# A fused transform and gated feed-forward kernel: the pair stage's order set anew, and the weight sums moved to the last two plain chunks

## The chip, the cores and the metric

The kernel runs on one core of one Trainium2 chip. The metric is the device time of one execution in microseconds. Three runs of the kernel before took 2718.64, 2719.53 and 2728.07 us, median 2719.53; the execution that was profiled took 2719.25 us, and its span, from its first instruction to its last, is 2717.5 us.

## The reference

```python
X = np.fft.rfft(x, axis=1)                       # x: 8 x 3008 x 256, fp32
Yr = Xr @ w_r - Xi @ w_i + b_r
Yi = Xr @ w_i + Xi @ w_r + b_i
Yr = np.sign(Yr) * np.maximum(np.abs(Yr) - 0.01, 0.0)     # Yi alike
y = np.fft.irfft(Yr + 1j * Yi, n=3008, axis=1)
t = y.reshape(24064, 256)
gate = 1 / (1 + np.exp(-(t @ w_gate)))           # 256 x 1536
out = (gate * (t @ w_val)) @ w_out               # 1536 x 256
```

A real Fourier transform along each of 8 sequences, a complex 256 x 256 mix with soft threshold in the frequency domain, the transform back, and a gated feed-forward layer over all 24064 tokens.

## The kernel before

**Numbers.** Products must be nearly exact in fp32. Most operands are therefore split into a high and a low part (type fp32r), and one 128 x 128 x 512 product is three matmuls, high x high, high x low and low x high (`products`, L1130 to 1133). The split costs a copy on ACT (high) and a subtraction on DVE (low) for every operand.

**Stages.** The sequences are transformed in groups of 1, 1, 2, 2 and 2. While the later groups are transformed, the feed-forward layer already runs on the first 4608 tokens, in 9 "plain" chunks of 512 tokens (`ffn`, a list of 9 x 12 units; unit j is chunk j // 12, hidden part j % 12). A unit is `ffn1` (12 matmuls `pg`, `pv`; ACT makes the sigmoid, DVE the product, ACT and DVE split it) and, two units behind, `ffn2` (6 matmuls `po`). The loop at L1045 places the transforms' steps (`side`) between the units by weights. Up to unit 87 all forward transforms and mixes are done (`part` = 108 - 20 = 88); then the transforms' memory (pools `cw` and `p2`, the latter with five 4 KB tiles of the tag `big`) is given up by `fft.close()` and the pool `p4` of the pair stage takes its place. In the last 20 units only inverse transforms are left: `load_v` (L479) loads a tile `vf` on SP's queue, two tiles in turn, `inv_a` multiplies it on PE (`pia`, 64 small matmuls, L502), and L514 stores the tokens to `yd` on SP's queue.

**The pair stage.** The other 19456 tokens go in 19 pairs of 512-token blocks. Each product of 2 x 2 blocks is made with 7 block products in place of 8 (a Strassen-Winograd scheme), for both weights. It needs sums of blocks of the weights and of the tokens:

- `make_t(fp, i)` (L684 to 697) makes the sums of the first weight for one hidden pair: 12 calls, additions on POOL in a scratch tile `tb`, split on POOL into `tr`, stored to the memory tensor `td`.
- `make_s(fp)` (L702 to 720) does it for the second weight: 6 calls, scratch `sa` and `sw`, split into `sr`, stored to `sd`. Scratch and results are tiles of the tag `big`.
- The token sums of a pair (`s1f`, `s2f`, and a difference written over `ypair`) are made on POOL too: by `first_operands` (L756 to 765) for the first pair, by `prepare` (L1189 to 1195) for the others.

The 18 weight steps stand in a list `sums`. The loop takes one after every third unit from unit 34 on, so they lie between the transforms.

In the pair stage a half step k multiplies one pair's operands `xop` with the sums `w1s` (loaded on SP from `td`, 4 buffers `w1s0` to `w1s3`): 7 products into the PSUM tiles `z`, `c` and `b`. ACT and DVE add them up, apply the gate and write `h`. Per 3 hidden pairs, `second` makes sums of `h` on POOL (L1298, and accumulating DMAs at L1292), splits them into `op` (ACT L1309, DVE L1311) and multiplies with `w2s` (loaded on SP from `sd`): 7 x 3 products into `l2z`. A pair is 12 half steps and two `second`: 12 x 7 + 2 x 21 = 126 products, 378 matmuls.

**What sets the order.** Outside the pair stage the framework orders each engine's instructions by its own estimate. Engines, SP's and POOL's DMA queues among them, take their instructions in that order, and a waiting instruction holds back what stands behind it. In the pair stage every instruction is a `Task` with an engine, a duration, a wished time `at` (shifted by an entry of the table `NUDGE`) and a latency. `arrange` (L185) plays the tasks through and emits them in the order in which they started. Tasks with `lock` (additions on POOL and subtractions on DVE that use two operands in SBUF) exclude each other in it: `lock` holds the time at which the last of them ended.

```python
starts = [(max(free[e], t.ready, lock if t.lock else 0.0), t) for t in ts]
...
if sums and j > 3 * NF - 3 and j % 3 == 1:
    sums.pop(0)()
```

The first three `w1s` (`load_w1`), the first pair's tokens (`load_y`) and `first_operands` are placed in the last plain chunk; the rest of the pair stage is placed by `arrange`.

Of the kernel before, what the change touches and what calls it, by code (L numbers as in the profile page):

```python
# [9 lines left out]
F32 = mybir.dt.float32  # L10
# [27 lines left out]
LAST_GAP, SIDE_GAP = 20, 3  # L38
PRE = 1
# [73 lines left out]
class Task:  # L113

    def __init__(self, eng, dur, at, fn, deps=(), lat=0.0, lock=False):
# [21 lines left out]
    ),  # L137
    "load": (
        230.81,
    ),  # L140
    "prepare": (
        -336.85, 397.58, 483.22, 32.48, 566.91, 83.5, 531.49, 56.76, 198.43, 398.39, 446.08, 4.74, 205.62,
        90.44, 533.23, 718.11, -102.53, 229.74, 96.65,
    ),
# [7 lines left out]
    ),  # L152
# [8 lines left out]
    ),  # L161
# [12 lines left out]
def arrange(tasks):  # L174

    left = {}
    users = {}
    ready = {e: [] for e in ENGINES}
    for t in tasks:
        t.deps = [d for d in dict.fromkeys(sum(t.behind, t.deps)) if d is not None and d is not t]  # L180
        left[t] = len(t.deps)
        for d in t.deps:
            users.setdefault(d, []).append(t)
        if not t.deps:
            t.ready = 0.0  # L185
            ready[t.eng].append(t)
    free = dict.fromkeys(ENGINES, 0.0)
    lock = 0.0
    order = []
    while True:  # L190
        best = None
        for e, ts in ready.items():
            if not ts:
                continue
            starts = [(max(free[e], t.ready, lock if t.lock else 0.0), t) for t in ts]
            first = min(b for b, _ in starts)
            b, t = min(((b, t) for b, t in starts if b <= first + WINDOW), key=lambda p: (p[1].at, p[0]))
            if best is None or b < best[0]:
                best = b, t
        if best is None:  # L200
            break
        b, t = best
        ready[t.eng].remove(t)
        t.start, t.end = b, b + t.dur * (1.0 if t.eng == "PE" else 1.02)
        free[t.eng] = t.end
        if t.lock:
            lock = t.end
        order.append(t)
        for u in users.get(t, ()):
            left[u] -= 1  # L210
            if not left[u]:
                u.ready = max(d.end + d.lat + hop(d, u) for d in u.deps)
                ready[u.eng].append(u)
    assert len(order) == len(tasks)
    return order
# [3 lines left out]
def tile_fft_mix_ffn(ctx: ExitStack, tc, x, w_r, w_i, b_r, b_i, w_one, w_out, mf, mi, mis, fa, ft, out):  # L219
# [457 lines left out]

    def make_t(fp, i):
        f0, f1 = 2 * fp, 2 * fp + 1
        g = nc.gpsimd  # L680
        w = big("tb").rearrange("p (a b) n -> p a b n", a=2)
# [8 lines left out]
        r = p2.tile([P, 4, 2, P], F32R, tag="big", bufs=NBIG, name="tr")  # L690
# [8 lines left out]
    def make_s(fp):  # L699
# [6 lines left out]
        w = big("sw").rearrange("p a n -> p (a n)").rearrange("p (k n) -> p k n", n=P)  # L706
# [9 lines left out]
        for k0, k1 in ((0, 4), (4, 7)):  # L716
            r = p2.tile([P, 4, 2, P], F32R, tag="big", bufs=NBIG, name="sr")[:, :k1 - k0]
# [309 lines left out]
    sums = [lambda fp=fp, i=i: make_t(fp, i) for fp in range(NH) for i in range(2)] + [lambda fp=fp: make_s(fp) for fp in range(NH)]  # L1027
    for j in range(NF, len(ffn)):
# [3 lines left out]
        if sums and j > 3 * NF - 3 and j % 3 == 1:  # L1032
            sums.pop(0)()
        while side and (acc >= side[0][0] or j >= (part if len(side) > n_last else end) - 1):
# [4 lines left out]
            if len(side) == n_last:  # L1039
# [4 lines left out]
                acc = 0.0  # L1044
        if c == NPL - 1:  # L1045
# [115 lines left out]
    def load_weights(k):  # L1161
        here[:] = "load", 0
        t = new_w1()
        w1_of[k] = t, task("SP", 0.5, (k - 1.5) * SLOT,
                           lambda: nc.sync.dma_start(t.get().bitcast(F32), td[k // 2 % NH, k % 2]), writes=[t], lat=7.5)

    def prepare(p):
# [11 lines left out]
        def sum_(at, fn, out, reads, deps):  # L1179
            return task("POOL", 1.5, (base + at) * SLOT, fn, reads=reads, writes=[out], deps=deps, lock=True)  # L1180

        def split(name, at, src, v, deps):
            t = new_x()
            hi = task("ACT", 0.63, (base + at) * SLOT, lambda: a_.copy(t.get()[:, 0], v()), reads=[src], writes=[t], deps=deps)
            lo = task("DVE", 0.69, (base + at) * SLOT + 1.0, lambda: sub(t.get()[:, 1], v(), t.get()[:, 0]),  # L1185
# [17 lines left out]
    def half(k):  # L1203
# [18 lines left out]
        def copied(at, deps):  # L1222
            t = new_tmp()
            return t, on("ACT", 0.6, at, lambda: a_.copy(t.get(), z.get()), [z], [t], deps)  # L1224
# [246 lines left out]
```

## Time and profile before

| what | value |
|---|---|
| median of 3 runs | 2719.53 us |
| the profiled execution, its span | 2719.25 us, 2717.5 us |
| PE, DVE, ACT, POOL busy | 98%, 80%, 63%, 38% of the span |
| last `yc` of the transforms made | 923.1 us |
| last 20 plain units | about 925 to 1029 us |
| first product of the pairs | 1028.9 us |
| one pair, from one wait of PE to the next | 88 us |

All times are microseconds from the start of the span. A row of a timeline gives start, length, engine, line, operation and tiles, and in brackets how long the engine was idle before and what ended that. `SPq` is SP's DMA queue: a row there is the issue of a transfer, not the transfer. A matmul's length in the trace is its way through the array; in a row of x3 the next product starts before the last one's end. A row of a window gives its length, then for PE, PEld (PE's weight loads), DVE, ACT and POOL the busy time and the count of instructions, then PE's granted clock, the share of the DMA engines and GB/s. A row of the groups gives count, busy time and mean, then idle time before and its causes.

### The profile page before, as it was taken

The page shows a single profiled execution, that of the slowest core. Times are in us where ns is not written, and L with a number is a line of the kernel's source. Part 1 is how long each engine was busy: PE and PEld are TensorE (multiplying, and loading weights), DVE is VectorE, ACT ScalarE, POOL GpSimd, SP SyncE. Part 2 cuts the span into 40 slices and gives each one's busy share as a digit, 9 for nine tenths or more (in the row PEclk, how much of TensorE's full clock was granted, in tenths as well). Part 3 has the DMA queues.
Part 4 walks back from the last instruction along what each step waited for, and adds up shares of the span by engine and source line. Part 5 has one row for each costly group of instructions (what it writes and reads, how often), then busy time and mean ns, then how long its engine had stood idle before and what let it go on. Part 6 is the DMA issues. An engine that isn't in the chain of part 4 may idle for free.

```text
span 2717.5 us, 45378 instructions
## 1 busy us (share of the span) xinstructions
PE 2660.2 (98%) x16763; PEld 2179.3 (80%) x16763; DVE 2173.0 (80%) x3100; ACT 1702.5 (63%) x2852; POOL 1046.1 (38%) x963
## 2 busy tenths in 40 slices
PE   9999999999899999999999999999999999999999
PEld 6778888887789888888888778788788788877777
DVE  5778888788788636888888888888888888887886
ACT  4565554554355446776777767776777667776765
POOL 1441012225700013445454455445554545444541
PEclk9999999999899999999999999999999999999999
DMA  9986655776655575787887778787878778777874
GB/s 299 290 284 194 194 150 171 206 213 209 201 162 150 169 225 163 242 264 222 261 257 242 240 243 270 237 253 233 270 238 252 227 256 261 245 239 224 270 228 138
DMA packets 257660, 617.83 MB, mean 227 GB/s; under 512 B 26464, under 2 KB 130656, under 8 KB 257440
## 3 DMA queue, kind: packets, MB, share of 16 engines
q1 hardware_dynamic: 222720, 521.29, 58.2%
q0 software_dynamic: 34608, 93.60, 15.1%
q8 instruction: 133, 2.18, 0.3%
q14 instruction: 87, 0.71, 0.1%
q10 hardware_dynamic: 112, 0.04, 0.0%
HBM read 440.50 MB, written 116.13 MB: 205 GB/s over the span
## 4 chain that ended last, share of the span: by engine, by line
PE 79%; DVE 13%; DMA 5%; issue 2%; ACT 1%; SPq 0%; POOL 0%; DVEq 0%; ACTq 0%; POOLq 0%
PE l2z L1133 17%; PE z L1133 17%; PE c L1133 10%; PE pm L425 5%; PE b L1133 4%; DVE op L1311 4%; PE pb L391 3%; DMA w2s<-sd 2%; PE pia L502 2%; DVE tmp L1227 2%; PE pg L555 2%; PE pg L556 2%; PE po L583 2%; PE pg L557 2%; PE pv L555 2%; PE pv L556 2%
## 5 line engine op out<-in xcount | busy, mean ns | idle before, releaser
L1133 PE MATMUL z<-xop,w1s 128*128 128x512 f32 x2592 | 682.0, 390 | 1.0 <-DMA w1s<-td 0.9
L1133 PE MATMUL l2z<-op,w2s 128*128 128x512 f32 x2331 | 594.4, 391 | 7.2 <-DMA w2s<-sd 5.0
L1133 PEld LDWEIGHTS z<-xop,w1s 128*128 128x128 f32 x2592 | 485.3, 188 | 108.0 <-DVE xop L1185 4.4
L1133 PEld LDWEIGHTS l2z<-op,w2s 128*128 128x128 f32 x2331 | 436.4, 188 | 108.4 <-issue 7.1
L1224 ACT COPY tmp<-z 128x512 f32<-128x512 f32 x684 | 398.1, 588 | 194.9 <-PE z L1133 112.3
L1311 DVE TENSOR_TENSOR op<-h,op 128x1024 fp32r<-128x1024 f32 (+1 forms) x444 | 463.3, 1070 | 39.1 <-ACT op L1309 36.7
L1309 ACT CAST op<-h 128x1024 fp32r<-128x1024 f32 (+1 forms) x444 | 360.3, 836 | 77.9 <-PE l2z L1133 68.7
L1133 PE MATMUL c<-xop,w1s 128*128 128x512 f32 x1296 | 351.4, 393 | 16.8 <-DVE tmp L1227 16.0
L1133 PEld LDWEIGHTS c<-xop,w1s 128*128 128x128 f32 x1296 | 241.0, 188 | 79.6 <-DVE tmp L1227 31.2
L1298 POOL TENSOR_TENSOR t<-h 128x512 f32<-128x512 f32 x111 | 166.2, 1497 | 330.4 <-DVE h L1263 329.3
L1227 DVE TENSOR_TENSOR tmp<-tmp,c 128x512 f32<-128x512 f32 x342 | 231.4, 679 | 26.5 <-ACT tmp L1224 15.6
L1271 POOL TENSOR_TENSOR h<-tmp 128x512 f32<-128x512 f32 x114 | 155.9, 1368 | 223.7 <-ACT tmp L1243 147.8
L1243 ACT ACTIVATE tmp<-tmp 128x512 f32<-128x512 f32 x342 | 215.2, 634 | 40.9 <-DVE tmp L1227 40.7
L1298 POOL TENSOR_TENSOR h<-h 128x512 f32<-128x512 f32 x111 | 183.0, 1649 | 7.2
L425 PE MATMUL pm<-w_sb,xsh 128*128 128x256 f32 x1008 | 184.3, 284 | 0.0
L1133 PE MATMUL b<-xop,w1s 128*128 128x512 f32 x648 | 182.6, 390 | 0.0
L1227 DVE TENSOR_TENSOR c<-tmp,c 128x512 f32<-128x512 f32 x114 | 79.1, 694 | 120.4 <-PE c L1133 120.1
L1292 POOL DMA_DIRECT2D h<-h x148 | 128.1, 900 | 85.0 <-ACT tmp L1224 44.6
L425 PEld LDWEIGHTS pm<-w_sb,xsh 128*128 128x128 f32 x1008 | 152.9, 189 | 0.8 <-ACT xsh L407 0.4
L1133 PEld LDWEIGHTS b<-xop,w1s 128*128 128x128 f32 x648 | 121.7, 188 | 25.5 <-DVE tmp L1227 0.3
L436 ACT CAST yh<-yc 128x512 fp32r<-128x512 f32 x84 | 52.1, 620 | 141.7 <-DVE yc L415 141.6
L425 PE MATMUL pm<-w_sb,xsl 128*128 128x256 f32 x504 | 139.5, 277 | 0.0
(199 smaller groups left out, 4989.3 us busy)
## 6 DMA issues: line engine op xcount, KB each, us to landing
w1s<-td SPq DMA_DIRECT2D x228, 896.0 KB, 6.3
w2s<-sd SPq DMA_DIRECT2D x259, 384.0 KB, 5.2
h<-h POOLq DMA_DIRECT2D x74, 512.0 KB, 7.7
zf<-zd SPq DMA_DIRECT2D x96, 256.0 KB, 3.7
vf<-vd SPq DMA_DIRECT2D x128, 192.0 KB, 4.1
vd<-vz SPq DMA_DIRECT2D x84, 256.0 KB, 2.9
ypair<-yd SPq DMA_DIRECT2D x19, 1024.0 KB, 7.7
out_dram<-acc SPq DMA_DIRECT2D x76, 256.0 KB, 6.0
```

The lines of the kernel that those rows point to most:

```text
L425: nc.tensor.matmul(o, l, r, start=(i == 0), stop=(i == len(mms) - 1))
L555: nc.tensor.matmul(t, wh, yth[:, ct], start=(ct == 0), stop=False)
L556: nc.tensor.matmul(t, wh, ytl[:, ct], start=False, stop=False)
L1133: nc.tensor.matmul(o, ws[i], vs[j], start=first and not i and not j, stop=i == 1, skip_group_check=not first)
L1224: return t, on("ACT", 0.6, at, lambda: a_.copy(t.get(), z.get()), [z], [t], deps)
L1227: return on("DVE", 0.69, at, lambda: add(t.get(), s.get(), o.get()), [x for x in (s, o) if x is not t], [t], deps)
L1243: return on("ACT", 0.64, at, lambda: a_.activation(t.get(), (o or t).get(), AF.Sigmoid), [o] if o else [], [t], deps)
L1271: made[3, q] = on("POOL", 1.5, 16, lambda: g_.tensor_mul(at_h(3), g22.get(), v.get()), [g22, v], [h], [d22, e22], True)
L1292: return [[on("POOL", 0.9, at + q0, lambda q0=q0, q1=q1: g_.dma_start(h.get()[:, dst, q0:q1], h.get()[:, src, q0:q1], accum_op=ALU.add), [ ...
L1298: return [[on("POOL", 1.5, at + q, lambda q=q: g_.tensor_sub(v()[:, q], h.get()[:, a, q], h.get()[:, b, q]), [h], [o], sum((d[q] for d in ...
L1309: hi = on("ACT", 0.2 + 0.43 * n, at - 8 + q0, lambda q0=q0, q1=q1: a_.copy(t.get()[:, 0, q0:q1], v()[:, q0:q1]), [t_in], [t], sum((d[i] fo ...
L1311: lo.append([on("DVE", 0.3 + 0.5 * n, at - 5 + q0, lambda q0=q0, q1=q1: sub(t.get()[:, 1, q0:q1], v()[:, q0:q1], t.get()[:, 0, q0:q1]), [t ...
```

## The change

It has two parts.

1. **The planner and its tables.** `arrange` no longer lets tasks with `lock` exclude each other. It plays in steps of time, and while DVE and POOL both run such a task, DVE goes at 0.47 and POOL at 0.8 of its speed. Durations and latencies are set anew (POOL's 1.5 becomes 1.3, DVE's 0.69 becomes 0.67 or 0.68, a `w1s` load 7.5 becomes 6.5, a `w2s` load 6.5 becomes 5.5), the time from one engine to another is shorter, and all entries of `NUDGE` are new (one row of it is shown below).
2. **The weight sums.** Their scratch and their results are no longer `big` tiles but buffers of the pair stage in `p4`: scratch in turn in `w1s3` and `w1s2`, results in `xop7` and `xop8`. They are made from unit 88 on, when `p4` is there, 18 steps in 15 units.

```diff
+SUMS_IN = 15
 NUDGE = {
...
     "load": (
-        230.81,
+        16.36,
     ),
...
+SHARED = {"DVE": 0.47, "POOL": 0.8}
 def hop(a, b):
     if a.eng == b.eng and not a.lat:
-        return 0.0 if a.eng == "PE" else 0.1
-    return 1.1 * (0.28 if a.eng == "PE" else 0.12)
+        return 0.0 if a.eng == "PE" else 0.05
+    return 1.1 * (0.22 if a.eng == "PE" else 0.07)
 def arrange(tasks):
...
+            first = min(max(t.ready, now) for t in ts)
+            t = min((t for t in ts if max(t.ready, now) <= first + WINDOW), key=lambda t: (t.at, t.i))
...
+        both = all(e in busy and busy[e][0].lock for e in SHARED)
+        rate = {e: SHARED[e] if both and e in SHARED else 1.0 for e in busy}
...
+    turns = [0]
+    def scratch():
+        turns[0] += 1
+        return p4.tile([P, 7 * 2 * P], F32, tag=f"w1s{2 + turns[0] % 2}", bufs=1, name="sums")
+    def rounded(k):
+        return p4.tile([P, 4, 2, P], F32R, tag=f"xop{7 + k}", bufs=1, name="hilo")
     def make_t(fp, i):
-        w = big("tb").rearrange("p (a b) n -> p a b n", a=2)
+        w = scratch()[:, :8 * P].rearrange("p (a b n) -> p a b n", a=2, b=2)
...
-        r = p2.tile([P, 4, 2, P], F32R, tag="big", bufs=NBIG, name="tr")
+        r = rounded(turns[0] % 2)
     def make_s(fp):
-        a = big("sa").rearrange("p a n -> p (a n)")[:, :4 * P].rearrange("p (f n) -> p f n", f=2)
+        t = scratch()
+        a = t[:, 8 * P:12 * P].rearrange("p (f n) -> p f n", f=2)
...
-            r = p2.tile([P, 4, 2, P], F32R, tag="big", bufs=NBIG, name="sr")[:, :k1 - k0]
+            r = rounded(k0 // 4)[:, :k1 - k0]
...
     for j in range(NF, len(ffn)):
         c, f = divmod(j, NF)
         ffn[j]()
         acc += rates[j >= part]
-        if sums and j > 3 * NF - 3 and j % 3 == 1:
-            sums.pop(0)()
...
+        if p4:
+            while sums and (n_sums - len(sums)) * SUMS_IN < n_sums * (j - part + 1):
+                sums.pop(0)()
```

**SP's queue in the last plain units.** Before, the first load of `w2s` stands among the loads of `vf` and the stores of `yd` like this (the sums had been stored long before):

```order
L479 DMA vf_12268<-vd7_99 48x1024 x2
L1320 DMA w2s_12995<-sd_102 128x768
L514 DMA yd_104<-yf_12305 128x2x188
L514 DMA yd_104<-yf_12308 128x2x188
L479 DMA vf_12346<-vd7_99 48x1024 x2
L593 DMA out_0_dram<-ot_12340 128x512
L593 DMA out_0_dram<-ot_12343 128x512
```

Now that load stands later in the queue, and the third load of `w1s` (into the buffer `w1s2`), which stood well ahead of this place before, comes after it:

```order
L1339 DMA w2s_12989<-sd_102 128x768
L485 DMA vf_12409<-vd7_99 48x1024
L520 DMA yd_104<-yf_12338 128x2x188
L520 DMA yd_104<-yf_12341 128x2x188
L485 DMA vf_12409<-vd7_99 48x1024
L485 DMA vf_12504<-vd7_99 48x1024
L520 DMA yd_104<-yf_12446 128x2x188
L520 DMA yd_104<-yf_12449 128x2x188
L485 DMA vf_12504<-vd7_99 48x1024
L752 DMA w1s_12752<-td_100 128x1792
L520 DMA yd_104<-yf_12541 128x2x188
L520 DMA yd_104<-yf_12544 128x2x188
```

Behind the `w2s` load stand the loads of the last five `vf` tiles, behind the `w1s` load those of the last three. The `w2s` load reads what the first three `make_s` store; the `w1s` load overwrites the scratch of the eighteenth step.

**POOL in the last plain units.** Before, the last step's stores (`sr` to `sd`) are followed by the four token sums of the first pair, and then by those of the second:

```order
L719 TENSOR_TENSOR sr_11220<-sw_11207,sr_11220 128x3x128
L720 DMA sd_102<-sr_11216 128x4x256
L720 DMA sd_102<-sr_11220 128x3x256
L756 TENSOR_TENSOR s1f_12533<-ypair_12311 128x512
L757 TENSOR_TENSOR s2f_12534<-s1f_12533,ypair_12311 128x512
L761 TENSOR_TENSOR ypair_12311<-ypair_12311 128x512
L765 TENSOR_TENSOR s2f_12534<-ypair_12311,s2f_12534 128x512
L1189 TENSOR_TENSOR s1f_13066<-ypair_12997 128x512
```

Now the sums of the weights (`sums`, split into `hilo`) reach into them; this is the end of the eighteenth step:

```order
L730 TENSOR_TENSOR sums_12734<-sums_12734 128x128
L778 TENSOR_TENSOR ypair_12177<-ypair_12177 128x512
L732 TENSOR_TENSOR sums_12734<-sums_12734 128x128
L735 CAST hilo_12748<-sums_12734 128x3x128
L782 TENSOR_TENSOR s2f_12471<-ypair_12177,s2f_12471 128x512
L736 TENSOR_TENSOR hilo_12748<-sums_12734,hilo_12748 128x3x128
L735 CAST hilo_12744<-sums_12734 128x4x128
L737 DMA sd_102<-hilo_12748 128x3x256
L736 TENSOR_TENSOR hilo_12744<-sums_12734,hilo_12744 128x4x128
L737 DMA sd_102<-hilo_12744 128x4x256
L1208 TENSOR_TENSOR s1f_13058<-ypair_12991 128x512
```

The last two token sums of the first pair (L778, L782) stand inside the last step; the first two (L773, L774) stand inside the third `make_s`. All twelve `make_t` stand ahead of them.

**POOL in the pair stage.** Before, the token sums of the next pair are spread between the sums of `h` (here in the second half of the first pair):

```order
L1292 DMA h_13827<-h_13827 128x1024
L1189 TENSOR_TENSOR s1f_14071<-ypair_13790 128x512
L1194 TENSOR_TENSOR ypair_13790<-ypair_13790 128x512
L1298 TENSOR_TENSOR t1_13901<-h_13827 128x512
L1271 TENSOR_TENSOR h_13827<-tmp_14078,tmp_14116 128x512
L1298 TENSOR_TENSOR h_13827<-h_13827 128x512
L1292 DMA h_13827<-h_13827 128x512
L1190 TENSOR_TENSOR s2f_14196<-s1f_14071,ypair_13790 128x512
```

Now three of the four stand in one run:

```order
L1317 TENSOR_TENSOR h_13369<-h_13369 128x512
L1311 DMA h_13369<-h_13369 128x512
L1208 TENSOR_TENSOR s1f_13801<-ypair_13725 128x512
L1209 TENSOR_TENSOR s2f_13820<-s1f_13801,ypair_13725 128x512
L1213 TENSOR_TENSOR ypair_13725<-ypair_13725 128x512
L1290 TENSOR_TENSOR h_13784<-tmp_13790,tmp_13834 128x512
```

The products of a pair, their number and their sizes stay.

More of the change, by code (lines that the diff above doesn't have):

```diff
@@ L164 @@
 ENGINES = ("PE", "ACT", "DVE", "POOL", "SP")
+SHARED = {"DVE": 0.47, "POOL": 0.8}
 def hop(a, b):
     if a.eng == b.eng and not a.lat:
-        return 0.0 if a.eng == "PE" else 0.1
-    return 1.1 * (0.28 if a.eng == "PE" else 0.12)
+        return 0.0 if a.eng == "PE" else 0.05
+    return 1.1 * (0.22 if a.eng == "PE" else 0.07)
 def arrange(tasks):
[L176 to L179, printed above, removed]
+    left, users = {}, {}
+    waiting = {e: [] for e in ENGINES}
+    busy = {}
+    for i, t in enumerate(tasks):
+        t.i, t.ready = i, 0.0
         t.deps = [d for d in dict.fromkeys(sum(t.behind, t.deps)) if d is not None and d is not t]
@@ L184, in arrange @@
         if not t.deps:
[L185 to L188, printed above, removed]
+            waiting[t.eng].append(t)
+    now = 0.0
     order = []
[L190 to L193, printed above, removed]
+    while len(order) < len(tasks) or busy:
+        wake = []
+        for e, ts in waiting.items():
+            if e in busy or not ts:
                 continue
[L195 to L214, printed above, removed]
+            first = min(max(t.ready, now) for t in ts)
+            t = min((t for t in ts if max(t.ready, now) <= first + WINDOW), key=lambda t: (t.at, t.i))
+            if t.ready > now + 1e-9:
+                wake.append(t.ready - now)
+                continue
+            ts.remove(t)
+            busy[e] = [t, t.dur]
+            t.start = now
+            order.append(t)
+        both = all(e in busy and busy[e][0].lock for e in SHARED)
+        rate = {e: SHARED[e] if both and e in SHARED else 1.0 for e in busy}
+        step = min(wake + [busy[e][1] / rate[e] for e in busy])
+        now += step
+        for e in list(busy):
+            busy[e][1] -= step * rate[e]
+            if busy[e][1] > 1e-9:
+                continue
+            t = busy.pop(e)[0]
+            t.end = now
+            for u in users.get(t, ()):
+                u.ready = max(u.ready, now + t.lat + hop(t, u))
+                left[u] -= 1
+                if not left[u]:
+                    waiting[u.eng].append(u)
     return order
@@ L1027, in tile_fft_mix_ffn @@
     sums = [lambda fp=fp, i=i: make_t(fp, i) for fp in range(NH) for i in range(2)] + [lambda fp=fp: make_s(fp) for fp in range(NH)]
+    n_sums = len(sums)
     for j in range(NF, len(ffn)):
@@ L1179, in sum_ @@
         def sum_(at, fn, out, reads, deps):
-            return task("POOL", 1.5, (base + at) * SLOT, fn, reads=reads, writes=[out], deps=deps, lock=True)
+            return task("POOL", 1.3, (base + at) * SLOT, fn, reads=reads, writes=[out], deps=deps, lock=True)
         def split(name, at, src, v, deps):
             t = new_x()
-            hi = task("ACT", 0.63, (base + at) * SLOT, lambda: a_.copy(t.get()[:, 0], v()), reads=[src], writes=[t], deps=deps)
-            lo = task("DVE", 0.69, (base + at) * SLOT + 1.0, lambda: sub(t.get()[:, 1], v(), t.get()[:, 0]),
+            hi = task("ACT", 0.625, (base + at) * SLOT, lambda: a_.copy(t.get()[:, 0], v()), reads=[src], writes=[t], deps=deps)
+            lo = task("DVE", 0.68, (base + at) * SLOT + 1.0, lambda: sub(t.get()[:, 1], v(), t.get()[:, 0]),
                       reads=[src], writes=[t], deps=[hi], lock=True)
@@ L1223, in copied @@
             t = new_tmp()
-            return t, on("ACT", 0.6, at, lambda: a_.copy(t.get(), z.get()), [z], [t], deps)
+            return t, on("ACT", 0.59, at, lambda: a_.copy(t.get(), z.get()), [z], [t], deps)
         def summed(at, t, s, o, deps):
-            return on("DVE", 0.69, at, lambda: add(t.get(), s.get(), o.get()), [x for x in (s, o) if x is not t], [t], deps)
+            return on("DVE", 0.67, at, lambda: add(t.get(), s.get(), o.get()), [x for x in (s, o) if x is not t], [t], deps)
         q1 = prod(0, z, "a11", "b11", True)
@@ L1266, in half @@
         d11 = summed(3.5, b, s, b, [ds, q2])
-        made[0, q] = on("DVE", 0.69, 4.6, lambda: mul(at_h(0), g11.get(), b.get()), [g11, b], [h], [d11, e11])
+        made[0, q] = on("DVE", 0.67, 4.6, lambda: mul(at_h(0), g11.get(), b.get()), [g11, b], [h], [d11, e11])
         v = new_tmp()
@@ L1335, in result @@
                 if s:
-                    return on("DVE", 0.69, at, lambda: add(t.get(), s.get(), o.get()), [s, o], [t], deps)
-                return on("ACT", 0.6, at, lambda: a_.copy(t.get(), o.get()), [o], [t], deps)
+                    return on("DVE", 0.67, at, lambda: add(t.get(), s.get(), o.get()), [s, o], [t], deps)
+                return on("ACT", 0.59, at, lambda: a_.copy(t.get(), o.get()), [o], [t], deps)
             before = [t.uses[-1]]
             if s:
-                before = [on("POOL", 1.5, at - 1, lambda: g_.tensor_add(t.get(), t.get(), s.get()), [s], [t],
+                before = [on("POOL", 1.3, at - 1, lambda: g_.tensor_add(t.get(), t.get(), s.get()), [s], [t],
                              before + list(deps[:1]), True)]
-            d = on("DVE", 0.69, at, lambda: add(t.get(), t.get(), o.get()), [o], [t], [*deps, *before])
+            d = on("DVE", 0.67, at, lambda: add(t.get(), t.get(), o.get()), [o], [t], [*deps, *before])
             ct, s_ = divmod(j, 2)
@@ L1421, in last_second @@
             t, o = results[p][j], os[2 * s_ + ct]
-            d = on("DVE", 0.69, 90, lambda t=t, o=o: add(t.get(), t.get(), o.get()), [o], [t], [d, t.uses[-1]])
+            d = on("DVE", 0.67, 90, lambda t=t, o=o: add(t.get(), t.get(), o.get()), [o], [t], [d, t.uses[-1]])
             col = T0 + (2 * p + s_) * HW
```

38 lines of the change are left out of this document (19 added, 19 removed), and 37 rows, old and new, of the table NUDGE.

## The prediction

> **What bounds the kernel now.** I read the page first, then the windows, the timeline around the last plain chunks, the waits and one period of the pair stage.
>
> ```profile
> core 0: 2717.5 us, clock 0.992
> ```
> ```profile
> PE 2660.2 (98%) x16763; PEld 2179.3 (80%) x16763; DVE 2173.0 (80%) x3100; ACT 1702.5 (63%) x2852; POOL 1046.1 (38%) x963
> ...
> POOL 1441012225700013445454455445554545444541
> ```
>
> PE is busy for 98% of the span, so time is gained only where it stands still or runs slowly, and lost wherever something new makes it stand. POOL has three empty slices of 68 us, from about 750 to 950 us: the weight sums end before them, and the pair stage begins after them. The change puts the sums at the end of that hole. The timeline says how much room there is: the third and fifth from the end of the plain stage's inverse transforms (`pia`), and the first product of the pairs.
>
> ```profile
> 995.26 1.20 PE L502 MATMUL pia<-ft_sb,vf 48*64 48x47 f32 x64
> ...
> 1006.08 1.15 PE L502 MATMUL pia<-ft_sb,vf 48*64 48x47 f32 x64
> ...
> 1028.93 0.84 PE L1133 MATMUL z<-a,w1s 128*128 128x512 f32 x3
> ```
>
> The next rows are windows (length, then busy time of PE, PEld, DVE, ACT and POOL, clock, DMA): the last plain units, and one pair.
>
> ```profile
> 925.00:1029.00 104.00, 104.00 (x1511) 83.82 (x1510) 34.82 (x48) 43.68 (x85) 8.48 (x6) 1.00 0.75 211
> 1147.80:1235.80 88.00, 86.96 (x379) 70.52 (x379) 74.74 (x97) 62.79 (x104) 44.18 (x33) 1.00 0.79 248
> ```
>
> From 925 to 1029 PE has no gap at all; POOL has 8.5 us of work and DVE 34.8 in 104 us. In a pair, DVE is busy for 75 of 88 us and POOL for 44, so the two overlap, and there PE waits once a pair for DVE:
>
> ```profile
> PE c L1133 <- DVE tmp L1227: 16.0, 17, 1.2
> ```
> ```profile
> 1235.77 0.96 PE L1133 MATMUL c<-xop,w1s 128*128 128x512 f32 x3 [0.92 <-DVE tmp L1227]
> ...
> 1237.94 0.84 PE L1133 MATMUL z<-xop,w1s 128*128 128x512 f32 x3
> 1238.62 0.84 PE L1133 MATMUL b<-xop,w1s 128*128 128x512 f32 x3
> ```
> ```profile
> 1230.73 1.55 DVE L1311 TENSOR_TENSOR op<-h,op 128x512 fp32r<-128x512 f32 x1
> ...
> 1235.64 0.68 DVE L1311 TENSOR_TENSOR op<-h,op 128x512 fp32r<-128x512 f32 x1
> ```
> ```profile
> 1231.80 1.64 POOL L1194 TENSOR_TENSOR ypair<-ypair 128x512 f32<-128x512 f32 x1
> ```
>
> One product is three matmuls and starts 0.68 us after the one before (1237.94 to 1238.62). A pair has 126 of them, 85.7 us; the window, cut from one such wait to the next, has 88.0 (the timeline gives 87.98). So 2.2 us a pair are lost, 42 us in 19 pairs, and no order can win more. The cause is in the last rows: the same DVE subtraction takes 0.68 us alone and 1.55 beside POOL's 1.64 us operation.
>
> **The sums in their new place.** They are the same 18 steps (12 for the first weight, 6 for the second), and each issues its own stores from POOL. What they cost is read where they ran back to back: two steps of the first kind, then two single steps of the second.
>
> ```profile
> 651.09:667.36 16.27, 16.27 (x163) 14.51 (x162) 15.18 (x20) 6.05 (x12) 15.79 (x22) 1.00 0.83 263
> 713.68:723.91 10.23, 4.01 (x70) 3.46 (x70) 8.80 (x10) 1.93 (x4) 10.07 (x15) 0.62 0.41 137
> 723.91:733.53 9.62, 8.31 (x34) 7.17 (x35) 4.64 (x4) 4.28 (x9) 9.47 (x15) 0.69 0.98 268
> ```
> ```profile
> L684 POOL TENSOR_TENSOR tb<-w1h,w1l x24: 729/748/1229, 352.9 to 660.3; 128x256 f32<-128x256 f32 x24
> L692 POOL CAST tr<-tb x24: 397/403/1132, 383.4 to 664.4; 128x256 fp32r<-128x256 f32 x24
> L693 POOL TENSOR_TENSOR tr<-tb,tr x24: 725/745/1225, 384.6 to 666.1; 128x256 fp32r<-128x256 f32 x24
> ...
> L687 POOL TENSOR_TENSOR tb<-tb x12: 454/640/1176, 355.6 to 661.6; 128x128 f32<-128x128 f32 x12
> ```
> ```profile
> L694 POOL DMA_DIRECT2D td<-tr x12 | 6.8, 568 | 3.3 <-POOL tr L693 3.3
> ```
>
> A step of the first kind took 8.1 us with DVE busy for 93% of the time. At the least values of its rows it takes 2 x (0.729 + 0.397 + 0.725) + 4 x 0.454 + 0.57 = 6.1 us, which I take as the price without DVE. DVE is busy for 33% in the last plain units, so I take 6.1 + 2.0 x 33/93 = 6.8. A step of the second kind took 10.2 us (DVE 86%) and 9.6 (DVE 48%); carried on to 33% that is 9.4. In POOL's order the pairs' first four operand sums stand among the last steps:
>
> ```profile
> 969.90 1.29 POOL L756 TENSOR_TENSOR s1f<-ypair 128x512 f32<-128x512 f32 x1 [236.37 <-DMA ypair<-yd]
> 971.26 1.62 POOL L757 TENSOR_TENSOR s2f<-s1f,ypair 128x512 f32<-128x512 f32 x1
> 972.84 1.74 POOL L761 TENSOR_TENSOR ypair<-ypair 128x512 f32<-128x512 f32 x1
> 975.82 1.29 POOL L765 TENSOR_TENSOR s2f<-ypair,s2f 128x512 f32<-128x512 f32 x1 [1.23 <-DVE s L753]
> ```
>
> They add 5.9 us. The whole is 12 x 6.8 + 6 x 9.4 + 5.9 = 144 us, while from the end of the transforms to the pairs there are 106.
>
> The GPSIMD Engine Reference of the Trainium skill (section 3.1) gives 2.6 cycles an element for an addition of two inputs on GpSimd at 1.2 GHz; an estimate from that page is 0.55 us for 256 elements, where the least row here has 0.729. With its figure for the eight two-input operations a first step would be 4.7 us and the sum below 25 us smaller; the measured rows decide.
>
> **When they start, and who waits.** The new buffers lie in memory that the transforms have used, and the first sum can start when the last `yc` is made:
>
> ```profile
> 922.38 0.69 DVE L415 TENSOR_TENSOR yc<-ys,yc 128x512 f32<-128x512 f32 x1
> ```
>
> That is 923.1. Nothing on PE waits for POOL there, but SP does. Its queue goes in order, and in the new order two loads stand in it that need the sums: the first `w2s`, which reads what three steps of the second kind store, and the third `w1s`, whose buffer is the scratch of the last step. Behind the first stand the `vf` loads for the last five inverse transforms (first used at 995.26), behind the second those for the last three (first used at 1006.08), and stores of `yd`. PE's matmuls of `pia` stand in PE's own order and wait for them. Prices:
>
> ```profile
> vf<-vd SPq DMA_DIRECT2D x128, 192.0 KB, 4.1
> ...
> sd<-sr POOLq DMA_DIRECT2D x6, 512.0 KB, 4.4
> ```
> ```profile
> 953.38 0.48 SPq L735 DMA_DIRECT2D w1s<-td  x1
> ...
> 955.71 1.12 SPq L479 DMA_DIRECT2D vf<-vd  x2
> ```
>
> From the issue of a `w1s` load to the end of the `vf` issues behind it SP needs 3.4 us (953.38 to 956.83), and 4.1 more for landing: 7.5 us.
> - First stop: 923.1 + 12 x 6.8 + 3 x 9.4 + 2.9 (two operand sums stand ahead) = 1035.8, + 4.4 for the store, + 7.5 = 1047.7 in place of 995.3: PE stands for 52 us.
> - The next unit takes 5.4 us (half of 995.26 to 1006.08), to 1053; the one after that finds its load behind the third `w1s`.
> - Second stop: the last step's last operation ends at 1035.8 + 3 x 9.4 + 3.0 - 0.8 (its store's issue) = 1066.2; + 7.5 = 1073.7 in place of 1006.1.
>
> So the plain stage ends **67.6 us later**. The stops do not add up; the second deadline contains the first. From below: at 6.1 us a first step it is 59. From above: at 8.1 and 10.2 us, 88. After that nothing of the sums is late: the third `w1s` needs only to land before the pairs start, which is then at 1096, and the operand sums lie ahead of the last step. Half clock after such a stop I put at 2 us (0 to 4): the last two windows above show clock 0.62 and 0.69 around stops of a few us.
>
> What lies under it costs nothing: DVE's 34.8 us in these units, stretched by 1.55/0.68, are 79 of 104. If that cover failed, PE would wait for `hl`, but it uses it two units later.
>
> **What the old place gives back.** There the sums stretched DVE's work and PE stood:
>
> ```profile
> 672.67 1.98 PE L338 MATMUL pd<-xd,ft_sb 47*64 47x512 f32 x6 [2.32 <-DVE yt L427]
> ```
> ```profile
> 716.33 0.55 PE L462 MATMUL pi<-yh,mi_sb 128*128 128x256 f32 x1 [4.55 <-issue]
> ...
> 718.52 0.45 PE L502 MATMUL pia<-ft_sb,vf 48*64 48x47 f32 x2 [0.57 <-DVE yt L427]
> 720.21 1.95 PE L502 MATMUL pia<-ft_sb,vf 48*64 48x47 f32 x62 [1.24 <-issue]
> 724.13 0.58 PE L462 MATMUL pi<-yh,mi_sb 128*128 128x256 f32 x1 [1.97 <-ACT yh L436]
> 725.81 0.58 PE L463 MATMUL pi<-yl,mi_sb 128*128 128x256 f32 x1 [1.10 <-DVE yl L437]
> ```
> ```profile
> 923.78 0.39 PE L462 MATMUL pi<-yh,mi_sb 128*128 128x256 f32 x1 [0.62 <-ACT yh L436]
> 924.50 0.39 PE L463 MATMUL pi<-yl,mi_sb 128*128 128x256 f32 x1 [0.34 <-DVE yl L437]
> ```
>
> The five waits from 716 to 726 are 9.4 us, and the slow clock in the two windows costs 4.01 x 0.38 + 8.31 x 0.31 = 4.1. The same place of the last transforms, with POOL idle, waits for 1.0. So 12.5 us go; of the 2.3 at 672 perhaps most: **-14 us** (-8 if the wait called "issue" stays, -17 if all goes).
>
> **The new order.** The rewritten planner, its durations and tables issue no instruction of their own; a pair keeps its 126 products. The planner's slowing of DVE to 0.47 and of POOL to 0.8 when both run is near the rows: 0.68/1.55 = 0.44, 1.29/1.64 = 0.79. The old planner held one of the two back, which the chip does not do. So the new order should foresee the wait of each pair; shorter hops and load times leave less slack for the DMAs. Nothing in the trace prices an order. It can win at most 42 us, less the products' own hiccups, say 38, and may lose 10 (a new wait of half a us a pair); I take the middle of what can be won, **-20 us**.
>
> **Sum.** 67.6 + 2 - 14 - 20 = +35.6. The profiled execution took 2719.25 us (span 2717.5), 0.3 under the median of 2719.53: **2755 us**.
>
> **Rivals.**
> - *The new order does nothing.* For it: the old one leaves only 2.2 us a pair. Then +55.6: 2775, and with sums at their upper price 2795.
> - *Faster: the sums fit.* With DVE mostly idle POOL's operations could be half as long. It decides when POOL reaches the third step's store by 995.3 - 7.5 - 4.4 = 983.4, 60 us after 923.1 in place of 113, and ends by 998.6, 75 us in place of 143. Then only -34 is left: 2685. Against it: the medians of L684 and L693, 0.748 and 0.745, lie on the least values, 0.729 and 0.725, so waiting for DVE is a small part. By the SBUF — State Buffer page of the Trainium skill ("Who interferes with whom") a DVE operation with two SBUF inputs and a reading GpSimd operation exclude each other for the whole instruction; that would favour this rival. The window from 651 speaks against it: DVE 15.18 and POOL 15.79 busy in 16.27 us.
> - *No change.* Sums at the floor (59), order near its limit (-36), all of the old stalls gone (-17): +6, 2725.
>
> **Numbers.** Forecast 0.62, its own range 2733 to 2770; order without effect 0.21; no change 0.10; faster 0.07. Half a per cent, 13.6 us, is about what a measurement of this kernel tells from no change. Slower by more: 0.83; within it 0.10; faster 0.07. A range from 2728 to 2790 leaves out the faster rival, half of "no change" and the sums at their upper price.
>
> **What would show it.** Right: SP idle for tens of us at the first `w2s` and again at the third `w1s`; PE waiting for `vf` near 995 for some 50 us and near 1053 for some 20; first product of the pairs near 1096; no five waits near 716; a period of about 87 us a pair. Wrong: `pia` waits of under 10 us there, or a pair of 88 us or more.

## The result, and the profile after

The changed kernel took 2752.4 us (median of four runs, 2746.26 to 2756.13), the kernel before 2720.2 in the same comparison (2718.64 to 2728.07): a ratio of 1.0116, with an interval from 1.0097 to 1.0136. It is slower by 32 us; the forecast was 2755. The profiled execution is the quickest of the four, 2746.26 with a span of 2744.4, so the traces lie 26.9 us apart where the medians lie 32.2. The terms below come from the traces.

The head of the page and the slices of POOL and of the clock:

```profile
span 2744.4 us, 45326 instructions
...
PE 2648.9 (97%) x16763; PEld 2182.5 (80%) x16763; DVE 2132.6 (78%) x3100; ACT 1687.9 (62%) x2852; POOL 981.1 (36%) x963
...
POOL 1431000000000992434544455445544455444532
PEclk9999999999999969999999999999999999999999
```

A slice is 68.6 us. POOL's hole now reaches from about 270 to 890 us, and two full slices follow it; in the second of them, 960 to 1029, the clock falls to 0.6.

Four rows of the timeline divide the difference: the last `yc` of the transforms, PE's two long stops behind it (in the second PE waits for a `vf` to land), and the first product of the pairs.

```profile
893.42 0.69 DVE L421 TENSOR_TENSOR yc<-ys,yc 128x512 f32<-128x512 f32 x1
...
992.98 0.79 PE L589 MATMUL po<-hh,w 128*128 128x512 f32 x1 [32.82 <-ACT ot L598]
...
1035.08 0.41 PE L508 MATMUL pia<-ft_sb,vf 48*64 48x47 f32 x2 [12.37 <-DMA vf<-vd]
...
1061.06 1.52 PE L1152 MATMUL c<-s,w1s 128*128 128x512 f32 x6
```

- The last `yc` comes at 893.4 in place of 922.4: the old place gave back **29.0 us**.
- From there to the first product 167.6 us pass in place of 106.5 (1028.93 - 922.38): the new place costs **61.1 us**.
- From the first product to the end of the span 1683.34 us remain in place of 1688.57: the new order is worth **5.2 us**.

-29.0 + 61.1 - 5.2 = 26.9, the difference of the spans.

PE's waits in the pair stage, first before, then after, say why the order is worth so little. (Columns: what waited, for what, total, times, longest.)

```profile
PE l2z L1133 <- DMA w2s<-sd: 5.0, 8, 2.2
```
```profile
PE l2z L1152 <- DMA w2s<-sd: 23.3, 13, 2.4
PE c L1152 <- DVE h L1284: 2.2, 5, 0.9
PE z L1152 <- ACT tmp L1243: 1.7, 4, 0.6
```

The 17 waits for DVE's `tmp`, 16.0 us, are gone, but the waits for the second weight's load grew from 5.0 us to 23.3. All of PE's waits there come to 23.8 us before and 27.9 after, so by these waits alone the new order would be the dearer one. Its 5.2 us stand in PE's busy time, 1650.9 us in place of 1659.1 for the same products; what shortened that is not shown.

### The profile page after: what moved, and what is told of

Its sections match the earlier page's. It is cut to its first block, busy times and chain, and to the rows that moved or that the text cites. A ratio compares the mean times of both kernels' runs of the same rounds, so it can differ in the third digit from the quotient of the medians.

```text
span 2744.4 us, 45326 instructions
## 1 busy us (share of the span) xinstructions
PE 2648.9 (97%) x16763; PEld 2182.5 (80%) x16763; DVE 2132.6 (78%) x3100; ACT 1687.9 (62%) x2852; POOL 981.1 (36%) x963
## 4 chain that ended last, share of the span: by engine, by line
PE 82%; DMA 8%; POOL 5%; DVE 3%; ACT 1%; issue 1%; SPq 0%; DVEq 0%; POOLq 0%; ACTq 0%
PE z L1152 21%; PE l2z L1152 18%; PE c L1152 10%; PE pm L431 6%; PE b L1152 5%; DMA w2s<-sd 4%; PE pb L397 3%; PE pia L508 2%; PE pg L561 2%; DMA ypair<-yd 2%; PE pg L562 1%; PE po L589 1%; PE pv L561 1%; PE pg L563 1%; PE pv L563 1%; PE pv L562 1%
## 5 line engine op out<-in xcount | busy, mean ns | idle before, releaser
L1152 PE MATMUL l2z<-op,w2s 128*128 128x512 f32 x2331 | 608.0, 391 | 23.3 <-DMA w2s<-sd 23.3
L1330 DVE TENSOR_TENSOR op<-h,op 128x1024 fp32r<-128x1024 f32 (+1 forms) x444 | 489.6, 1121 | 73.2 <-ACT op L1328 68.7
L1152 PE MATMUL c<-xop,w1s 128*128 128x512 f32 x1296 | 358.8, 391 | 2.5 <-DVE h L1284 2.2
L1290 POOL TENSOR_TENSOR h<-tmp 128x512 f32<-128x512 f32 x114 | 168.8, 1481 | 375.3 <-DVE tmp L1246 297.9
L700 POOL TENSOR_TENSOR sums<-w1h,w1l 128x256 f32<-128x256 f32 x24 | 18.5, 772 | 618.8 <-DVE yc L421 618.8
L1317 POOL TENSOR_TENSOR t<-h 128x512 f32<-128x512 f32 x111 | 144.2, 1299 | 151.0 <-DVE h L1282 147.0
L1317 POOL TENSOR_TENSOR h<-h 128x512 f32<-128x512 f32 x111 | 155.7, 1403 | 8.7
L1359 POOL TENSOR_TENSOR acc<-acc,tmp 128x512 f32<-128x512 f32 x54 | 90.9, 1683 | 86.4 <-ACT tmp L1348 86.4
```

Source lines behind the costliest of these rows:

```text
L1152: nc.tensor.matmul(o, ws[i], vs[j], start=first and not i and not j, stop=i == 1, skip_group_check=not first)
L1290: made[3, q] = on("POOL", 1.3, 16, lambda: g_.tensor_mul(at_h(3), g22.get(), v.get()), [g22, v], [h], [d22, e22], True)
L1317: return [[on("POOL", 1.3, at + q, lambda q=q: g_.tensor_sub(v()[:, q], h.get()[:, a, q], h.get()[:, b, q]), [h], [o], sum((d[q] for d in ...
L1330: lo.append([on("DVE", 0.13 + 0.555 * n, at - 5 + q0, lambda q0=q0, q1=q1: sub(t.get()[:, 1, q0:q1], v()[:, q0:q1], t.get()[:, 0, q0:q1]), ...
L1359: before = [on("POOL", 1.3, at - 1, lambda: g_.tensor_add(t.get(), t.get(), s.get()), [s], [t], before + list(deps[:1]), True)]
```

## The experiments

Times are medians, against a median of the kernel before on the same chip of 2718.2 us (order_only, place_only, operands_late, one_scratch), 2716.8 (no_sums, split10, split_w1, w1_behind), 2719.4 (split_late, w1_between, both) and 2721.5 (late_fixed).

### The two parts apart

The new order with the sums as they were; and the old order with the sums as they are now:

```
# order_only: the changed kernel, with the loop's lines and both functions as before
+        if sums and j > 3 * NF - 3 and j % 3 == 1:
+            sums.pop(0)()
-        if p4:
-            while sums and (n_sums - len(sums)) * SUMS_IN < n_sums * (j - part + 1):
-                sums.pop(0)()
# place_only: the kernel before, with the same lines the other way round
```

> The changed kernel with the sums of weights in their old place and old buffers: the new order alone. Theory (from the two traces: from the first product of the pairs to the last, 1684.2 us before and 1679.2 after): the order is worth 5 us, so 2720.2 - 5 = 2715; PE's 16.0 us of waits for DVE's tmp are gone, and some 20 us of waits for w2s stand in their place. Rival (the prediction's term): the order is worth 20 us and the profiled runs hide it, 2700. Second rival: the order wins only beside the new place, 2720 or more.

Measured 2714.5, a ratio of 0.9985 (0.9973 to 0.9997). PE's waits in the pair stage:

```profile
PE l2z L1140 <- DMA w2s<-sd: 23.0, 14, 2.0
```

> The kernel before with the sums in their new place and buffers and its old order of the pairs: the move alone. Theory: the old place gives back 28.6 us (the last transforms end that much earlier), the new one costs 60.7, so 2720.2 + 32.1 = 2752, 5 us of which the new order would then win back or which the runs can't tell; I say 2752 to 2757. Rival (the prediction's terms, -14 and +69.6): 2776. PE waits as in the changed kernel: some 33 us near 960 behind an ACT copy, some 12 near 1035 for vf.

Measured 2750.5, just under the 2752 to 2757 that were expected; a ratio of 1.0128 (1.0109 to 1.0148). The waits in the last plain units:

```profile
PE po L584 <- ACT ot L593: 32.4, 1, 32.4
PE pia L503 <- ACT s L764: 10.6, 1, 10.6
```

Order alone -4, place alone +32: the terms of the traces, and neither of the prediction's two, -20 and +55.6 (69.6 - 14). The loss is the move's, and the order brings next to nothing with the old place as with the new.

### Which queue holds PE

The prediction named SP's queue. The trace of after names ACT at the first stop:

```profile
989.75 0.62 ACT L769 CAST s<-s1f 128x512 fp32r<-128x512 f32 x1 [35.69 <-POOL s1f L773]
```
```profile
988.47 1.25 POOL L773 TENSOR_TENSOR s1f<-ypair 128x512 f32<-128x512 f32 x1
...
1024.52 1.27 POOL L736 TENSOR_TENSOR hilo<-sums,hilo 128x512 fp32r<-128x512 f32 x1
```

ACT's copy of the first operand sum stands 35.7 us for POOL, which reaches that sum behind fourteen steps and most of a fifteenth; behind the copy, in ACT's queue, stand the plain stage's copies `ot`, `hh` and `yf`, for which PE waits. The third `w1s` load goes out at 1025.82, when POOL's last operation has ended (1024.52 + 1.27). Two edits were to take away one hold each (a hold is a waiting copy or load that keeps what stands behind it from PE):

```
# one_scratch
-        return p4.tile([P, 7 * 2 * P], F32, tag=f"w1s{2 + turns[0] % 2}", bufs=1, name="sums")
+        return p4.tile([P, 7 * 2 * P], F32, tag="w1s3", bufs=1, name="sums")
# operands_late: the operands' sums and copies are called after the loop
-            if prep and f > 2:
-                prep.pop(0)()
```

> The changed kernel with the copies and sums of the first pair's operands called after the last plain unit in place of within the last chunk; nothing else. Theory (two deadlines, of which the later contains the first): PE's stop of 32.8 us near 960, in which ACT's copy of an operand sum waited for POOL, goes; PE then runs on to a vf load near 972 that SP's queue holds behind the first w2s load until about 995, and the last three vf loads still wait for the third w1s load: the pairs start as before and the time stays at 2752, within 4. Rival: the stops add, 36 us less: 2716.

Measured 2748.8, a ratio of 1.0122 (1.0103 to 1.0140): nothing gained, as the theory had it. ACT's copy no longer stands there, and SP's queue and PE show what stood behind it:

```profile
963.89 0.50 SPq L485 DMA_DIRECT2D vf<-vd  x1
1000.64 0.34 SPq L1337 DMA_DIRECT2D w2s<-sd  x1
```
```profile
1004.86 0.41 PE L508 MATMUL pia<-ft_sb,vf 48*64 48x47 f32 x2 [29.94 <-DMA vf<-vd]
...
1061.55 1.52 PE L1150 MATMUL c<-s,w1s 128*128 128x512 f32 x6
```

This is the prediction's first stop: SP issues nothing for 36 us, until the first `w2s` load can go, and PE waits 29.9 us for the `vf` behind it. It had been in the changed kernel all along, covered by ACT's. The pairs start at 1061.55, within 0.5 us of after.

> The changed kernel with one scratch buffer for the sums (that of the fourth w1s) in place of two, so that the third w1s load no longer waits for the last step; nothing else. Theory (two stops, the second held by that load): the first stop near 960 stays, the second near 1035 goes with its 13.0 us and the 2.9 us of slow clock behind it: 2752.4 - 16 = 2736. Rival: vf is late anyway because the w2s load ahead of it holds SP, or the steps, which can no longer overlap, end later: less than 5 us gained, 2748 or more.

Measured 2755.2, a ratio of 1.0137 (1.0119 to 1.0155): the theory failed. The third `w1s` load went out at 924, but PE stopped again near the end, for ACT, and POOL's last sum came later:

```profile
1036.45 0.62 ACT L769 CAST a<-ypair 128x512 fp32r<-128x512 f32 x1 [18.12 <-DMA sd<-hilo]
```
```profile
1037.49 0.80 PE L561 MATMUL pg<-yth,w1h 128*128 128x512 f32 x1 [10.94 <-ACT yf L519]
```
```profile
1034.21 1.27 POOL L736 TENSOR_TENSOR hilo<-sums,hilo 128x512 fp32r<-128x512 f32 x1
```

The operand `a` goes into one of the two buffers in which the sums are rounded, so its copy waits for the stores of the last step. And with one scratch buffer the steps no longer overlap: POOL ends at 1035.5 in place of 1025.8. That is the second half of the rival; the first, `vf` behind the `w2s` load, cost 5.9 us. The edit changes two things at once, so it doesn't price the third `w1s` load alone. At least four holds lead from POOL's sums to PE: an operand sum and an operand buffer through ACT's queue, a `w2s` and a `w1s` load through SP's. In operands_late, taking one away uncovered the next; in after, place_only, operands_late and one_scratch the pairs start 27 to 37 us after POOL's last sum of the weights.

### What the old place costs

> The new order with the sums of weights left out: copies of the weights are stored where the sums should be, by POOL's queue and without an operation of POOL, so the output is not the reference's. It prices the old place: theory (the last transforms end 28.6 us earlier once the sums are gone from there), 2714.5 - 28.6 = 2686. Rival (the prediction's 12.5 to 17 us, the rest of the 28.6 coming from something else in the move): 2698 to 2702.

```
     def make_t(fp, i):
...
+        for n, f in enumerate((f0, f1)):
+            for v, w in enumerate((w1h, w1l)):
+                g.dma_start(td[fp, i][:, 3 + 2 * n:5 + 2 * n, v], w[:, f, i].bitcast(F32))
```

Measured 2712.3, a ratio of 0.9975 (0.9962 to 0.9989), where 2686 was expected. The total can't decide: the copies went out in the first 210 us, where DMA is at its densest, and delayed PE there by 20.8 us. One matmul ahead of the old place and one behind it, in the run with the new order alone and in this one:

```profile
191.16 0.40 PE L561 MATMUL pg<-yth,w1h 128*128 128x512 f32 x1
...
726.13 0.40 PE L563 MATMUL pg<-yth,w1l 128*128 128x512 f32 x1
```
```profile
211.91 0.40 PE L561 MATMUL pg<-yth,w1h 128*128 128x512 f32 x1
...
721.82 0.39 PE L563 MATMUL pg<-yth,w1l 128*128 128x512 f32 x1
```

A run that was 20.8 us behind at 211 us is 4.3 ahead at the second: the sums cost 25.1 us in their old place. In after, which has the sums elsewhere, that second matmul stands at 701.01, again 25.1 us ahead of order_only, and 28.6 ahead of before (729.60). So some 25 of the 29.0 are the sums', and the rest lies between two traces that both have the sums in the old place; the 12.5 to 17 of the prediction are too few either way.

### Fewer steps late

Ten of the twelve steps of the first kind go back to the old place and its buffers; two and the six of the second kind stay late, with one scratch buffer:

```
+FIRST = 10
...
+        if len(sums) > n_sums - FIRST and j > 3 * NF - 3 and j % 3 == 1:
+            sums.pop(0)()
...
-            while sums and (n_sums - len(sums)) * SUMS_IN < n_sums * (j - part + 1):
+            while sums and (n_sums - FIRST - len(sums)) * SUMS_IN < (n_sums - FIRST) * (j - part + 1):
```

> The new order; the first ten steps of the sums in their old place and buffers, the other eight in the new place with one scratch buffer. Theory (the ten early steps, spaced three units apart, cost little, since before 667 us the kernel before had lost only 8 us by them; POOL then needs 2 x 6.1 + 6 x 8.9 + 5 = 71 us after the transforms, less than the 72 to the first load that would be held and the 106 to the pairs): 2714.5 - 28.6 + 8 = 2694. Rival (operand sums, w2s load and operand buffers still come behind the sums in the queues, so that eight steps hold PE as eighteen do, for about 8/18 of the time): 2686 + 8 + 27 = 2721.

Measured 2724.8, a ratio of 1.0027 (1.0013 to 1.0041). The first half of the theory held (the last `yc` came 20.3 us earlier than with the order alone, 20.6 expected), the second did not: ACT's copy stood for `s1f` again, and PE with it.

```profile
977.03 0.62 ACT L770 CAST s<-s1f 128x512 fp32r<-128x512 f32 x1 [23.55 <-POOL s1f L774]
```
```profile
978.07 0.79 PE L562 MATMUL pg<-yth,w1h 128*128 128x512 f32 x1 [22.07 <-ACT yf L520]
```

> The kernel with ten steps early and eight late, and the copies and sums of the first pair's operands called after the last plain unit. Theory (eight steps are done within 84 us of the end of the transforms, and what held PE for 22.1 us in the run with ten and eight was only ACT's copy of an operand sum, queued ahead of the plain stage's copies): the stop goes, the pairs start near 1008 in place of 1034.9, and 2724.8 - 27 = 2698. Rival (the hold only moves, as with one scratch buffer: to SP's w2s load or to the pairs' first operands): 2712 or more.

The edit is that of operands_late, in this kernel. Measured 2722.0, a ratio of 1.0011 (1.0001 to 1.0020). The theory failed. The edit did not do here what it had done there: called later, the copy kept its place in ACT's queue, since the plain stage's order is the scheduler's.

```profile
980.77 0.62 ACT L770 CAST s<-s1f 128x512 fp32r<-128x512 f32 x1 [26.22 <-POOL s1f L774]
```

### The load that is late in the pairs

With the new order alone, where PE waits for `w2s`: SP's queue, the wait, and the time from the load's issue to its landing.

```profile
1194.36 0.32 SPq L1172 DMA_DIRECT2D w1s<-td  x1
1195.04 0.42 SPq L1327 DMA_DIRECT2D w2s<-sd  x1
1195.55 0.39 SPq L1183 DMA_DIRECT2D ypair<-yd  x1
1196.03 15.07 SPq L1172 DMA_DIRECT2D w1s<-td  x3
```
```profile
1203.65 1.66 PE L1140 MATMUL l2z<-op,w2s 128*128 128x512 f32 x6 [1.54 <-DMA w2s<-sd]
```
```profile
DMA to landing us min/median/max: 8.6/8.6/8.6
```

The first row and the three that follow it within 2 us are four loads, 3.2 MB together (the last row merges three). The `w2s` load lands after 8.6 us, where the new plan counts on 5.5 (the old one had 6.5); the median of all `w2s` loads is 4.2. Two runs move the `w1s` load that stands ahead, in SP's queue alone:

```
         order = arrange(tasks)
+        sp = [t for t in order if t.eng == "SP"]
+        for n in range(2, len(sp)):
+            if [t.load for t in sp[n - 2:n + 1]] == ["w1", "w2", "y"]:
+                order.remove(sp[n - 2])
+                order.insert(order.index(sp[n]) + 1, sp[n - 2])   # w1_between: without + 1
```

> The new order with the sums in their old place, and in SP's queue, at each of the places where w1s, w2s and ypair are loaded within 1.2 us of each other, the w1s load put behind the ypair load; nothing else. Theory (the w2s load takes 8.7 us there in place of 5.5 because the 896 KB of w1s lie ahead of it, and PE waits 1.5 to 2.4 us for it): w2s lands some 3 us earlier, the waits of about 20 us go, 2714.5 - 18 = 2697. Rival (ypair and POOL's own transfers slow it, or something else is late next): within 5 us of 2714.5.

Measured 2704.7, a ratio of 0.9952 (0.9939 to 0.9964). Half of the gain came: the waits for `w2s` are gone, and the load that was moved is late by about 1 us. PE's waits from 1150 to 2600 us:

```profile
PE z L1141 <- DMA w1s<-td: 16.0, 16, 1.8
```

> The new order with the sums in their old place, and the w1s load put between the w2s load and the ypair load in place of behind ypair; nothing else. Theory (each load lands when those ahead of it in the queue have; behind ypair the w1s load came 0.7 to 1.8 us too late at 17 places): w1s lands some 3 us earlier, w2s still in time, the 16.6 us of waits for w1s go: 2704.7 - 14 = 2691. Rival (the four loads share the same bytes a second and one is late in any order): within 5 us of 2704.7, or up to 2714.

Measured 2693.3, a ratio of 0.9904 (0.9890 to 0.9918). With `w2s`, `w1s`, `ypair` in that order the same `w2s` load lands after 5.9 us, and from 1150 to 2600 us no load is late by more than 0.2:

```profile
PE z L1141 <- ACT tmp L1235: 4.4, 12, 0.8
PE z L1141 <- DMA w1s<-td: 0.2, 1, 0.2
```

### A version that beats both

The ten early steps and the `w1s` load behind `ypair` at once (the run split_w1, for which 2676 was expected) measured 2714.1, a ratio of 0.9990 (0.9978 to 1.0001). That is 10.7 below split10, as w1_behind is 9.8 below order_only: the two edits add, but each had brought less than its theory, and ACT's copy still held PE for 21.4 us.

> Both edits at once: ten steps early and eight late with the first operands called last, and the w1s load between w2s and ypair. Theory: they lie in different stages and add: 2714.5 - 16.5 - 23.5 = 2675. Rival (as far as either edit falls back by its own rival): 2690 to 2705.

Measured 2703.2, a ratio of 0.9941 (0.9928 to 0.9954): ten steps early and the `w1s` load between, where 2675 was expected. ACT's copy still stood (22.3 us of PE), so this half was as in split_late, and the load's half held. The last run ties the operands' calls to the last three plain units:

```
+        if j < len(ffn) - LATE:
+            ffn[j]()
+        else:
+            with tc.manual_schedule():
+                ffn[j]()
+                for _ in range(3):
+                    if prep:
+                        prep.pop(0)()
```

> Ten steps early and eight late, the w1s load between w2s and ypair, and the sums and copies of the first pair's operands tied to the last three plain units, so that ACT's copies really stand behind the plain stage's (in the two runs with those calls moved to the end they had kept their place in ACT's queue). Theory (ACT's copy of an operand sum, waiting for POOL's eight steps, is all that held PE there for some 22 us): the stop of 22 us near 955 goes, with 3 us of slow clock behind it; the copies among the last units cost up to 5 us; 2703.2 - 20 = 2683, 10 below the 2693.3 of the run with the sums in their old place and the w1s load between. Rival (SP's first w2s load, which waits for the third step of the second kind and has vf loads behind it, holds PE in ACT's place): 2695 or more.

Measured 2683.1, a ratio of 0.9871 (0.9850 to 0.9893), 10 us below w1_between, which has all the sums in their old place. The copies now come at 1001 us, the stop is gone, and the pairs start at 1008.1:

```profile
1001.45 0.61 ACT L771 CAST a<-ypair 128x512 fp32r<-128x512 f32 x1
```
```profile
PE pia L510 <- DMA vf<-vd: 4.3, 4, 2.7
```
```profile
1008.09 1.52 PE L1161 MATMUL c<-s,w1s 128*128 128x512 f32 x6
```

## Why the prediction was right, step by step

The time and the sign were right, and so was the mechanism of the largest term: the sums don't fit between the transforms and the pairs, and POOL's lateness reaches PE through queues that go in order. Three terms were mis-sized, and their errors largely cancel: the sums 8.5 too dear, the old place 11 to 15 too cheap, the order 15 too good. That the forecast of 2755 lies within 3 us of the median is therefore luck; the traces' 26.9 stands against the sum's 35.6.

- **Sums in the new place, 69.6 with the clock; measured 61.1.** POOL ran from 894.35 to 1025.8, 131 us, where the step had 143. The 12 steps of the first kind took 6.0 us each, the price at the least values, not 6.8 with a share for DVE; the six of the second 9.0, less the operand sums, not 9.4.
- **"Nothing on PE waits for POOL there, but SP does": the step that failed.** The operand sums were counted as POOL's time, but not that ACT copies them and that the plain stage's copies stand behind those. PE stopped at 960, some 12 us ahead of the place that was named (995.3, less the 23 by which PE was early there), and for 36 us, not 52; the stop that was named lay behind it, as operands_late showed.
- **The stops do not add, and the end is set by the end of the last step: right.** With the first stop's cause gone the pairs started at 1061.55 in place of 1061.06. But the third `w1s` load was not the only hold at the end; the operand buffers were another.
- **Clock after the stops, 2 us: too small.** From 993.0, where PE goes on, to 1003.4 the clock is 0.50. In a window table (length, busy PE, PEld, DVE, ACT, POOL, clock, DMA):

```profile
993.00:1000.00 7.00, 3.88 (x31) 2.31 (x34) 7.00 (x5) 1.86 (x4) 6.98 (x13) 0.50 0.57 197
1000.00:1003.40 3.40, 3.40 (x55) 2.92 (x50) 3.01 (x2) 0.36 (x1) 3.40 (x6) 0.51 1.01 266
1003.40:1010.00 6.60, 6.60 (x89) 5.28 (x89) 2.21 (x3) 3.57 (x8) 6.24 (x11) 1.00 1.01 313
```

  PE is busy for 7.3 us of these 10.4, at half speed: 3.6 us lost. Behind the second stop some 3 more go: from 1035.08 to 1045 PE is busy for 9.3 us at a clock of 0.71.
- **The old place, -14; measured -29.0 against before, -25.1 by no_sums and against order_only.** Only the stop at 672 and those from 711 on had been counted, and the slow clock behind the latter alone. The same windows of the kernel before and of after:

```profile
450.00:500.00 50.00, 47.32 (x400) 38.21 (x400) 38.52 (x65) 24.30 (x44) 11.25 (x17) 0.94 0.54 163
650.00:700.00 50.00, 47.51 (x495) 38.10 (x494) 43.76 (x58) 21.37 (x40) 45.79 (x67) 0.93 0.70 221
700.00:750.00 50.00, 40.50 (x399) 35.74 (x397) 38.32 (x52) 18.09 (x32) 31.26 (x48) 0.86 0.65 193
```
```profile
450.00:500.00 50.00, 49.77 (x438) 41.96 (x437) 36.89 (x67) 25.89 (x47) 0.00 (x0) 1.00 0.60 171
650.00:700.00 50.00, 49.49 (x657) 42.66 (x656) 37.42 (x68) 25.04 (x46) 0.00 (x0) 1.00 0.54 156
```

  Standing and clock together, the three windows of before lost 5, 5 and 15 us more than those of after: each of the first two 2 to 2.5 us of standing and some 3 of slow clock, the last 9.5 and 5.7 (in after PE is busy there throughout, at full clock). That is 26 of the 29.
- **The order, -20; measured -5 in the trace and -4 in order_only.** That it takes the DVE wait away was right. The 20 was the middle of a range without a row, and late loads, which the text had named as a risk, took its place: the median pair still takes 88.0 us, the value that the text gave as a sign of being wrong. Whether the shorter load times in the tables or only the order of the loads made `w2s` late, no run separates. With the loads in another order the new plan brought what had been hoped for: w1_between lies 21 us below order_only (2714.5 to 2693.3) and 26 below before.
- **The signs.** Right: the five waits near 716 are gone, and SP issues nothing from 1010.2 until the third `w1s` load at 1025.82. Not so: SP's first long stretch without an issue ends with the store of `ot`, for which ACT's queue was late, and not with the `w2s` load; no wait for `vf` of 50 us came near 995, and the pairs start at 1061 and not near 1096.
- **The faster rival** needed POOL's operations at half their time. They ran at the least values of before and no lower. The Trainium skill's SBUF — State Buffer page ("Who interferes with whom"), which spoke for it, has issue order decide which of the two engines blocks. The trace of operands_late doesn't bear that out: DVE paid, though its subtraction began at 1019.66, ahead of three of the POOL operations that it stood through (1019.81, 1021.03 and 1021.97; last section).

## What to carry to other kernels

Before moving work to an idle engine, list every instruction of the other engines that waits for it, and for each what stands behind it in its own queue: an ACT copy and a DMA load that nobody needs yet can hold work that is needed at once. Sum the work against the hole first; if it doesn't fit, moving less of it may, once the waiting copies stand late (split10 lost, late_fixed won). And price a stall with the slow clock behind it, and a planned load with what is issued beside it.

## What was not expected of the hardware

A DVE operation can stand through several of POOL's. In operands_late the subtraction that takes 0.68 us alone took 3.46 and 3.32, and each time ended only in a pause of POOL, while POOL issued a store:

```profile
1019.66 3.46 DVE L770 TENSOR_TENSOR s<-s1f,s 128x512 fp32r<-128x512 f32 x1 [48.31 <-ACT s L769]
1023.04 3.32 DVE L770 TENSOR_TENSOR s<-s2f,s 128x512 fp32r<-128x512 f32 x1
```
```profile
1019.81 1.25 POOL L774 TENSOR_TENSOR s2f<-s1f,ypair 128x512 f32<-128x512 f32 x1
1021.03 0.98 POOL L736 TENSOR_TENSOR hilo<-sums,hilo 128x384 fp32r<-128x384 f32 x1
1021.97 0.60 POOL L735 CAST hilo<-sums 128x512 fp32r<-128x512 f32 x1
1022.52 0.77 POOL L737 DMA_DIRECT2D sd<-hilo  x1
...
1024.54 1.26 POOL L778 TENSOR_TENSOR ypair<-ypair 128x512 f32<-128x512 f32 x1
1025.74 0.79 POOL L737 DMA_DIRECT2D sd<-hilo  x1
```

The first ends at 1023.12, after the cast that ends at 1022.57; the second at 1026.36, after the addition that ends at 1025.80. The prediction had taken 1.55 us, one operation's delay, as the price; a dense run of POOL's operations can cost more.
